# Attention scores: queries and keys as two fp32r parts in the lower and upper half of the array's rows, issued in pairs of heads

## The chip, the cores and the metric

One core of a Trainium2 chip runs the whole program. The metric is the device time of one execution in microseconds (us). A matmul here is an instruction of TensorE (PE): it multiplies a stationary operand, loaded first by a weight load (PEld), with a moving operand that streams through, and writes into one of eight PSUM banks. VectorE (DVE), ScalarE (ACT) and GpSimd (POOL) do the rest, SyncE (SP) issues most DMAs.

## The reference

Two independent results are put side by side: an attention with a memory over four segments, and a filter in the frequency domain (a real 2-D FFT of 2048 x 576, a product with a complex weight, and the inverse).

```python
q,k,v = x@wq, x@wk, x@wv            # 2048 x 576, 32 heads of 18, segments of 512
for s in range(4):
    qs, ks, vs = q[:, :, s], k[:, :, s], v[:, :, s]
    logits = einsum("bhqd,bhkd->bhqk", qs, ks) * scale + mask    # causal within the segment
    p = softmax(logits); a_dot = einsum("bhqk,bhkd->bhqd", p, vs)
    pq = phi(qs); num = pq @ M; den = (pq . z) + 1e-6
    outs.append(g * num / den + (1 - g) * a_dot)
    pk = phi(ks); M += pk^T vs; z += sum(pk)
a = concat(outs) @ wo
b = irfft2(rfft2(x2) * (w_r + 1j*w_i))
```

Everything is asked for in fp32. The kernel gets there by splitting operands into parts that TensorE takes in one pass and summing the products of the parts.

## The kernel before, in words

The program is written out in one order for all engines; each engine runs its own instructions in that order. It has these stages: the forward transform; the projections (`projections`, with the middle of the transform on DVE between its steps); the inverse transform, with a `prologue` of the attention beside it; the attention loop (`attention`, line 928 on); the last projection.

**Projections.** For each of 4 segments nine units `qk_unit` (line 467) make 128 rows of q and k each: 14 matmuls of width 512 (line 464) into a PSUM bank `pj`, then the result is split into three bf16 parts in `sp3` (three buffers): a copy on ACT (477), a subtraction on DVE in PSUM (484), a second copy on ACT (488), and the rest either by a subtraction on DVE (490, 18 units) or by a matmul with a negative identity `nid` and a third copy on ACT (492, 493, 18 units). A DMA on SP's queue writes the three parts to DRAM (`qkD`, line 494). Four `v_unit` per segment follow.

**Stacks.** For eight heads (a group n of 16) `stack_dmas` loads six pieces of 18 rows each for q and for k: q as parts 0,0,0,1,1,2 and k as 0,1,2,0,1,0, so that one matmul over 108 rows sums the six products of parts that matter. Rows 108 and 109 hold the row maxima (for q) and -1 (for k). There are three q and four k buffers.

**Scores.** A step t of the attention loop is one head: quad k = t//4, head hh = t%4 in it. Scores are made twice. `s1` (line 636) makes them with queries on the partitions for the head t+10: four matmuls (widths 384, 128, 512, 256) and one bf16 matmul that adds the causal mask to two diagonal blocks; DVE takes row maxima from them (648, 654). `mpath` turns the maxima of four heads by a transpose on PE (674) and a small DMA into rows 108 and 109 of q. `s2` (line 680) makes the scores again with keys on the partitions for the head t, maxima already subtracted, and ACT takes the exponential (689, 694, 698); POOL masks the diagonal blocks after every fourth head (701). `s1` and `s2` are generators of three steps each, which the loop calls in turn, with other work between them: `pv` (line 718, P times V, in 32-column strips), and in some stages of the loop the memory products (`mem1`, `combine`) and the output projection (`oproj`, line 861) from a queue `bg`. PSUM banks: three for `s1`, three for `s2`, one `pv`, one `post`. The prologue makes `s1` of the first ten heads.

What sets the order around the change: the order in which the loop calls these generators, the rings of three PSUM banks, and SP's queue for the stack loads, of which the loop takes two per step.

## Time and profile before

| | |
|---|---|
| timed runs | 707.5, 711.49, 711.28 us (median 711.28) |
| profiled execution | span 709.2 us from its first to its last instruction; the page gives no other time of it |
| granted TensorE clock | 0.997 |
| HBM | 81.78 MB read, 38.24 MB written |
| DMA share of the span | hardware queue 51.8%, software queue 8.2% |

Busy times are sums of durations, and matmuls overlap, so the distance between the starts of neighbouring instructions tells the cost of one better than its duration. Rows of a timeline give the start in us, the duration, the engine, the line, what is written and read and the shape; a bracket says how long the engine was idle before and what ended it. Rows of windows give the stretch, its length, and then for each engine the busy time with the number of instructions, the granted clock, the DMA share and GB/s.

### The profile page before, as it was taken

The page shows a single profiled execution, that of the slowest core. Times are in us where ns is not written, and L with a number is a line of the kernel's source. Part 1 is how long each engine was busy: PE and PEld are TensorE (multiplying, and loading weights), DVE is VectorE, ACT ScalarE, POOL GpSimd, SP SyncE. Part 2 cuts the span into 40 slices and gives each one's busy share as a digit, 9 for nine tenths or more (in the row PEclk, how much of TensorE's full clock was granted, in tenths as well). Part 3 has the DMA queues.
Part 4 walks back from the last instruction along what each step waited for, and adds up shares of the span by engine and source line. Part 5 has one row for each costly group of instructions (what it writes and reads, how often), then busy time and mean ns, then how long its engine had stood idle before and what let it go on. Part 6 is the DMA issues. An engine that isn't in the chain of part 4 may idle for free.

```text
span 709.2 us, 14168 instructions
## 1 busy us (share of the span) xinstructions
PE 676.4 (95%) x4861; PEld 498.7 (70%) x4861; DVE 556.2 (78%) x1233; ACT 441.0 (62%) x994; POOL 208.8 (29%) x409
## 2 busy tenths in 40 slices
PE   4999999999999999999999899999999999998997
PEld 4999779889879888999844444444566445764677
DVE  6999999899989889887588688877666876568153
ACT  3657695574574563444388677777666676567741
POOL 2110000100100111565165334555233753246210
PEclk9999999999999999999999999999999999999999
DMA  9876546555563568899647666676556765441331
GB/s 343 272 233 205 150 141 194 175 178 167 165 211 133 165 215 279 201 239 211 180 109 176 172 161 154 173 181 169 128 129 185 171 164 128 122 129 52 99 100 69
DMA packets 83388, 121.04 MB, mean 171 GB/s; under 512 B 11368, under 2 KB 50902, under 8 KB 83180
## 3 DMA queue, kind: packets, MB, share of 16 engines
q1 hardware_dynamic: 76724, 104.11, 51.8%
q0 software_dynamic: 6592, 16.03, 8.2%
q8 instruction: 38, 0.62, 0.4%
q14 instruction: 34, 0.28, 0.1%
HBM read 81.78 MB, written 38.24 MB: 169 GB/s over the span
## 4 chain that ended last, share of the span: by engine, by line
PE 61%; DVE 9%; DMA 6%; ACT 5%; issue 3%; POOL 3%; DVEq 0%; SPq 0%; ACTq 0%; POOLq 0%
PE pv L718 9%; PE po L861 7%; PE pj L464 6%; PE pjv L464 6%; PE s L644 5%; PE i L300 4%; PE i L311 4%; PE s L652 3%; PE s L688 3%; PE po L892 2%; DVE junk L648 2%; PE s L692 2%; PE pn L791 2%; PE pm L524 2%; PE s L653 2%
## 5 line engine op out<-in xcount | busy, mean ns | idle before, releaser
L648 DVE CUSTOM_DVE_ANT_0 junk<-s,mask 128x512 bf16<-128x512 f32 (+1 forms) x256 | 141.8, 554 | 55.1 <-PE s L644 44.3
L654 DVE TENSOR_REDUCE mx<-s 128x4 f32<-128x512 f32 x128 | 87.9, 687 | 20.0 <-PE s L653 18.2
L689 ACT ACTIVATE P<-s 128x512 f32<-128x512 f32 x128 | 77.2, 603 | 24.1 <-PE s L688 20.9
L718 PE MATMUL pv<-P,vs 128*32 128x512 f32 (+3 forms) x1024 | 82.3, 440 | 0.0
L694 ACT ACTIVATE P<-s 128x512 f32<-128x512 f32 x128 | 77.1, 602 | 6.9 <-PE s L693 3.8
L698 ACT ACTIVATE P<-s 128x256 f32<-128x256 f32 x128 | 49.6, 387 | 49.7 <-PE s L697 49.6
L701 POOL TENSOR_SCALAR_AFFINE_SELECT P<-P 128x512 f32<-128x512 f32 x116 | 69.4, 635 | 5.6 <-ACT P L689 4.7
L718 PEld LDWEIGHTS pv<-P,vs 128*32 128x32 f32 x1024 | 26.9, 109 | 45.0 <-issue 42.9
L464 PE MATMUL pj<-x,wqkh 128*128 128x512 f32 x162 | 56.1, 407 | 0.0
L210 DVE TENSOR_TENSOR t<-Z 128x580 f32<-128x580 f32 x64 | 46.7, 757 | 0.2
L514 POOL MEMSET vt<- 128x32 f32 x16 | 2.4, 159 | 148.8 <-PE pm L524 121.5
L210 DVE TENSOR_TENSOR Z<-t 128x580 f32<-128x580 f32 x64 | 45.9, 756 | 0.0
L644 PE MATMUL s<-Ks,Qs 108*128 108x512 bf16 (+1 forms) x128 | 42.2, 330 | 0.0
L488 ACT CAST sp<-pj 128x512 bf16<-128x512 f32 x36 | 21.1, 585 | 30.7 <-DVE pj L484 30.7
L142 PE MATMUL f<-ftab,eh 128*128 128x290 f32 (+1 forms) x160 | 31.6, 317 | 9.0 <-DMA ftab<-ftab 9.0
L300 PE MATMUL i<-civ,Y 128*128 128x256 f32 (+1 forms) x288 | 37.9, 284 | 1.6 <-DVE T L332 1.6
L300 PEld LDWEIGHTS i<-civ,Y 128*128 128x128 f32 (+1 forms) x288 | 35.8, 181 | 1.8 <-DVE T L332 1.8
L311 PE MATMUL i<-itab,T 128*128 128x290 f32 (+1 forms) x224 | 36.4, 312 | 0.0
L464 PEld LDWEIGHTS pj<-x,wqkh 128*128 128x128 f32 x162 | 30.4, 188 | 8.4 <-issue 1.7
L669 POOL CAST mh<-mg 128x16 bf16<-128x16 f32 x32 | 6.8, 214 | 99.1 <-ACT mg L667 67.9
L464 PE MATMUL pj<-xh,wqkh 128*128 128x512 f32 x90 | 35.6, 395 | 0.0
L464 PE MATMUL pj<-xh,wqkl 128*128 128x512 f32 x90 | 35.6, 395 | 0.0
(214 smaller groups left out, 1859.6 us busy)
## 6 DMA issues: line engine op xcount, KB each, us to landing
qkD<-sp SPq DMA_DIRECT2D x36, 384.0 KB
Ks<-qkD SPq DMA_DIRECT2D x72, 144.0 KB
x<-qkD SPq DMA_DIRECT2D x60, 144.0 KB
Qs<-qkD SPq DMA_DIRECT2D x60, 144.0 KB
xin<-xb SPq DMA_DIRECT2D x16, 384.0 KB
cfw<-cfw POOLq DMA_DIRECT2D x16, 384.0 KB, 4.5
civ<-civ POOLq DMA_DIRECT2D x16, 384.0 KB, 7.5
vs<-vD SPq DMA_DIRECT2D x16, 330.0 KB
```

The lines of the kernel that those rows point to most:

```text
L210: v.tensor_tensor(o,a,b,op=op)
L300: nc.tensor.matmul(p[:m,k],Y[i][:,q,c*128:c*128+m],cc[:,hl,o:o+256],start=n==0,stop=n==5)
L311: nc.tensor.matmul(p,x,t,start=n==0,stop=n==6)
L464: s.nc.tensor.matmul(out,a,b,start=i==0,stop=i==len(L)-1)
L644: nc.tensor.matmul(out,Q[:108,h,128*i:128*i+128],K[:108,h,:128*(i+1)],start=True,stop=True)
L648: nc.vector.tensor_tensor_reduce(out=junk[:,:w],in0=src,in1=s.mask[:,512-w:],scale=1.0,scalar=-3.0e38, op0=OP.add,op1=OP.max,accum_out=s.m ...
L654: nc.vector.tensor_reduce(out=s.mx[k][:,hh],in_=pa.rearrange("p (b c) -> p b c",c=128),axis=mybir.AxisListType.X,op=OP.max)
L689: nc.scalar.activation(P[0][:,hh],p0,AF.Exp,scale=SC)
L694: nc.scalar.activation(P[1][:,hh],p1,AF.Exp,scale=SC)
L701: if k<29: nc.gpsimd.affine_select(out=x,in_=x,pattern=pat+[[1,128]],compare_op=OP.is_ge,fill=0.0,base=0,channel_multiplier=-1)
L718: nc.tensor.matmul(s.pvt[32*hh:32*hh+32,128*j:],vt[:,j,19*h:19*h+32],mv[0][:,hh,mv[1]],start=j==0,stop=j==2,skip_group_check=True)
L861: nc.tensor.matmul(ps,a[t][:r,c],b[:r,t,w],start=i==0,stop=i==14)
```

## The change

q and k are split into two fp32r parts instead of three bf16 parts, with one copy on ACT and one subtraction on DVE; the `nid` matmuls, the second and third copies are gone. `sp` has two buffers of 4 KB per partition instead of three of 3 KB. A stack now has three pieces of 18 rows (q parts 0,0,1; k parts 0,1,0), 54 rows, plus two for maxima and -1. The first quad of a group lies in rows 0 to 55, the second in rows 64 to 119, and pieces of four heads are loaded instead of eight (as many DMAs of as many bytes). The scores of head t (`s2` before, B) and of head t+12 (`s1` before, A; t+10 before) always lie in different halves of the rows; `pair` issues their four products in turn, B and A of equal width, 512, 384, 128 and 256, then the mask product, then ACT's and DVE's work on them. `pv` and the background steps come after a whole pair. `mpath` starts after the quad's fourth head and its transpose follows the next pair; its PSUM bank is now that of `pv`. The prologue makes A alone for twelve heads.

```diff
-        s.qkD=[d(f"qkD{i}",[1152,3,512],BF) for i in range(4)]
+        s.qkD=[d(f"qkD{i}",[1152,2,512],F32) for i in range(4)]
...
-    def third(s,g,mt): return g>0 and mt%3
     def qk_unit(s,g,mt,tp,pp):
...
         ps=pp.tile([128,512],F32,name="pj",tag="pj")
         yield from s.passes(ps,g,"wqk",slice(128*mt,128*mt+128),slice(0,512),False)
         yield
-        sp3=tp.tile([128,3,512],BF,name="sp3",bufs=3)
+        sp=tp.tile([128,2,512],F32R,name="sp",bufs=2)
...
-        nc.scalar.copy(sp3[:,0],ps)
...
+        nc.vector.tensor_tensor(sp[:,1],ps,sp[:,0].bitcast(F32),op=OP.subtract)
         if r1>r0: nc.vector.scalar_tensor_tensor(e[r0:r1],ps[r0:r1],0.0,e[r0:r1],op0=OP.max,op1=OP.add)
-        nc.vector.tensor_tensor(ps,ps,sp3[:,0],op=OP.subtract)
         qr=min(r1,128 if mt<4 else (64 if mt==4 else 0))
         if qr>r0: nc.sync.dma_start(s.pqD[g][128*mt:128*mt+qr],e[:qr])
         yield
-        nc.scalar.copy(sp3[:,1],ps)
-        yield
-        if s.third(g,mt): nc.vector.tensor_tensor(sp3[:,2],ps,sp3[:,1],op=OP.subtract)
-        else:
-            nc.tensor.matmul(ps,s.nid,sp3[:,1],start=False,stop=True,skip_group_check=True)
-            nc.scalar.copy(sp3[:,2],ps)
-        nc.sync.dma_start(s.qkD[g][128*mt:128*mt+128],sp3)
+        nc.sync.dma_start(s.qkD[g][128*mt:128*mt+128],sp.bitcast(F32))
...
-        s.nid=wv.tile([128,128],BF,name="nid"); s.nc.scalar.activation(s.nid,s.ident,AF.Copy,scale=-1.0)
...
-                w=tot/(36-18*.3+12*2.7+4*2.0)*((2.7 if g<3 else 2.0) if i>8 else .7 if s.third(g,i) else 1.0)
+                w=tot/(36+12*2.7+4*2.0)*((2.7 if g<3 else 2.0) if i>8 else 1.0)
...
-        s.Qs+=[cp.tile([128,8,512],BF,name=f"Qs{i}") for i in range(1,3)]
-        s.Ks+=[cp.tile([128,8,512],BF,name=f"Ks{i}") for i in range(1,4)]
+        s.Qs+=[cp.tile([128,4,512],F32R,name=f"Qs{i}") for i in range(1,3)]
+        s.Ks+=[cp.tile([128,4,512],F32R,name=f"Ks{i}") for i in range(1,4)]
...
-        t=pool.tile([128,18,512],BF,name="x0",tag="x0",bufs=1)
-        s.Qs,s.Ks=[t[:,:8]],[t[:,8:16]]; s.loaded=set()
+        t=pool.tile([128,9,512],F32R,name="x0",tag="x0",bufs=1)
+        s.Qs,s.Ks=[t[:,:4]],[t[:,4:8]]; s.loaded=set()
...
+    def stack_dmas(s,n,qk,halves=(0,1)):
 
...
-        T,base,order=((s.Qs[n%3],0,(0,0,0,1,1,2)),(s.Ks[n%4],576,(0,1,2,0,1,0)))[qk]
-        for pc,o in enumerate(order):
-            a=s.qkD[g][base+8*G*18:base+8*G*18+18,o]
-            ap=bass.AP(tensor=a.tensor,offset=a.offset,ap=[[1536,18],[1536*18,8],[1,512]])
-            def go(T=T,pc=pc,ap=ap):
-                nc.sync.dma_start(T[18*pc:18*pc+18],ap)
-                if pc==5: s.loaded.add((n,qk))
-            L.append(go)
+        T,base,order=((s.Qs[n%3],0,(0,0,1)),(s.Ks[n%4],576,(0,1,0)))[qk]
+        for qd in halves:
+            for pc,o in enumerate(order):
+                a=s.qkD[g][base+(8*G+4*qd)*18:base+(8*G+4*qd)*18+18,o]
+                ap=bass.AP(tensor=a.tensor,offset=a.offset,ap=[[1024,18],[1024*18,4],[1,512]])
+                def go(T=T,r=64*qd+18*pc,ap=ap,pc=pc,qd=qd):
+                    nc.sync.dma_start(T[r:r+18].bitcast(F32),ap)
+                    if pc==2: s.loaded.add((2*n+qd,qk))
+                L.append(go)
         return L
...
-    def s1(s,t):
...
+    def pair(s,a,b):
+
+        nc=s.nc; A=[];B=[]
...
+            k,hh=divmod(a,4); n,qd=divmod(k,2); r=64*qd
+            assert (k,0) in s.loaded and (k,1) in s.loaded,a
+            Q,K=s.Qs[n%3][r:r+54,hh],s.Ks[n%4][r:r+54,hh]
...
+            pc,pa=[s.ps1.tile([128,512],F32,name="s1",tag="s1") for _ in range(2)]; pb=s.ps1.tile([128,256],F32,name="s1",tag="s1")
+            A=[(pc,3,512,True),(pa[:,:384],2,384,True),(pa[:,384:],0,128,False),(pb,1,256,True)]
+            A=[(o,Q[:,128*i:128*i+128],K[:,:w],f) for o,i,w,f in A]
...
+            u,hb=divmod(b,4); n,qe=divmod(u,2); r=64*qe
+            q,kk=s.Qs[n%3][r:r+56,hb],s.Ks[n%4][r:r+56,hb]
...
+            p0,p1=[s.ps.tile([128,512],F32,name="s2",tag="s2") for _ in range(2)]; p2=s.ps.tile([128,256],F32,name="s2",tag="s2")
+            B=[(p0,0,128*0),(p1[:,:384],1,128),(p1[:,384:],3,384),(p2,2,256)]
+            B=[(o,kk[:,128*j:128*j+128],q[:,c:],True) for o,j,c in B]
+        for i in range(4):
+            for L in (B,A):
+                if not L: continue
+                o,x,y,f=L[i]
+                nc.tensor.matmul(o,x,y,start=f,stop=L is B or i in (0,3),skip_group_check=True)
+        if A:
+            nc.tensor.matmul(pa[:,256:].rearrange("p (a c) -> p a c",a=2),s.idb,s.tri[:,None,:].to_broadcast([128,2,128]),start=False,stop=True,skip_group_check=True)
+        if B:
+            nc.scalar.activation(P[0][:,hb],p0,AF.Exp,scale=SC)
+            nc.scalar.activation(P[1][:,hb],p1,AF.Exp,scale=SC)
+            nc.scalar.activation(P[2][:,hb],p2,AF.Exp,scale=SC)
+        if A:
+            def red(src,i):
+                w=128*(i+1)
+                junk=s.sm.tile([128,512],BF,name="junk",bufs=1)
+                nc.vector.tensor_tensor_reduce(out=junk[:,:w],in0=src,in1=s.mask[:,512-w:],scale=1.0,scalar=-3.0e38,
+                    op0=OP.add,op1=OP.max,accum_out=s.mg[k][:,hh,i:i+1])
+            red(pc,3); red(pb,1)
+            nc.vector.tensor_reduce(out=s.mx[k][:,hh],in_=pa.rearrange("p (b c) -> p b c",c=128),axis=mybir.AxisListType.X,op=OP.max)
+        if B and hb==3:
+            def sel(x,pat):
...
-        p,a=(s.ps,"post") if 1<k<10 else (s.psm,s.mtag)
-        pt=p.tile([128,1024],BF,name="mt",tag=a)[:,:128]
+        pt=s.psm.tile([128,1024],BF,name="mt",tag=s.mtag)[:,:128]
         nc.tensor.transpose(pt,mh.rearrange("p a m -> p (a m)"),s.idb)
         yield
         mt=s.sm.tile([32,128],BF,name="mts",bufs=1)
         nc.scalar.copy(mt,pt[:32])
-        nc.gpsimd.dma_start(Q[108:110,4*qd:4*qd+4].rearrange("p h (i c) -> p (h i) c",c=128),mt)
...
+        a="post" if s.now<117 else "s1" if s.now<131 or name=="po" else "s2"
...
-        i=0
-        for t in range(10):
-            for _ in s.s1(t):
-                for _ in range(1+(i%24==0)):
-                    if q: q.pop(0)()
-                i+=1
+        m=None
+        for t in range(12):
+            s.pair(t,None)
+            if 2<=t<6:
+                for r in (54,118): nc.gpsimd.dma_start(s.Ks[t-2][r:r+2].rearrange("p h c -> p (h c)"),io["neg1"][:,:2048])
+            for i in range(3):
+                if q: q.pop(0)()
+                if m is not None and i<2: next(m,None)
                 yield
-            if 2<=t<6: nc.gpsimd.dma_start(s.Ks[t-2][108:110].rearrange("p h c -> p (h c)"),io["neg1"])
-            if t in (3,7): m=s.mpath(t//4); next(m)
-            if t in (4,8): next(m); next(m,None)
-        assert not q
+            m=None
+            if t%4==3: m=s.mpath(t//4); next(m)
+        while q: q.pop(0)()
+        if m is not None:
+            for _ in m: pass
...
-        nc=s.nc; s.tp,s.ps,s.psm,s.mtag=tp,ps,s.ps1,"s1"
+        nc=s.nc; s.tp,s.ps,s.psm,s.mtag=tp,ps,ps,"pv"
...
-            if hh==0 and qd==0:
-                if 0<n<14: q+=s.stack_dmas(n+2,0)
-                if 0<n<13: q+=s.stack_dmas(n+3,1)
-                if n+2<16: q.append(lambda n=n: s.load_v(n+2))
+            if hh==0 and k>0:
+                if k+5<32: q+=s.stack_dmas((k+5)//2,0,((k+5)%2,))
+                if k+7<32: q+=s.stack_dmas((k+7)//2,1,((k+7)%2,))
+            if hh==0 and qd==1 and n+2<16: q.append(lambda n=n: s.load_v(n+2))
...
-            a=s.s1(t+10) if t+10<128 else iter(())
-            b=s.s2(t) if t<128 else iter(())
             if q: q.pop(0)()
             if qu: qu.pop(0)()
-            if hh==3 and m is not None: steps(m,1)
-            steps(a,1)
-            steps(b,1)
+            if t<128: s.pair(t+12 if t+12<128 else None,t)
+            if hh==0 and m is not None: steps(m,1)
             r=(t-5)%4
+            if 5<=t<129: s.pv((t-5)//4,(t-5)%4)
+            if hh==3 and k+3<32: m=s.mpath(k+3); next(m)
             if r%2: run_bg(1)
-            steps(a,1)
-            steps(b,1)
-            if 5<=t<129: s.pv((t-5)//4,(t-5)%4)
+            if hh==0 and m is not None: steps(m,1)
...
-            steps(a,1)
-            steps(b,1)
-            if hh==2 and m is not None: steps(m,1)
-            if hh==1 and k+2<32: m=s.mpath(k+2); next(m)
```

PE in the quiet part of the attention loop (`idb` and `tri` make the mask product, `s` are score banks, `x` is the first q or k stack). Before, from the mask product of one head to the P·V of a quad:

```order
L653 LDWEIGHTS idb
L653 MATMUL s_5022<-tri,idb 128x256
L688 LDWEIGHTS Ks_3179
L688 MATMUL s_5027<-Qs_3177,Ks_3179 128x512 [waits Activation_49]
L644 LDWEIGHTS x_2655
L644 MATMUL s_5030<-Ks_3180,x_2655 128x512 [waits DVE_49]
L692 LDWEIGHTS Ks_3179
L692 MATMUL s_5034<-Qs_3177,Ks_3179 128x384 [waits Activation_49]
L693 LDWEIGHTS Ks_3179
L693 MATMUL s_5034<-Qs_3177,Ks_3179 128x128
L718 MATMUL pv<-P_4852,vs 32x512 [waits Pool_49]
L718 MATMUL pv<-P_4852,vs 32x512 x3
```

Each product has a weight load of its own, and first scores (644, 652) and second scores (688 to 697) take turns; P·V stands before the last two products of the head. Now, one head and the P·V after it:

```order
L653 MATMUL s_4897<-Qs_3081,Ks_3083 128x512 [waits Activation_49]
L653 MATMUL s_4894<-Ks_3084,x_2583 128x512 [waits DVE_49]
L653 MATMUL s_4898<-Qs_3081,Ks_3083 128x384 [waits Activation_49]
L653 MATMUL s_4895<-Ks_3084,x_2583 128x384 [waits DVE_49]
L653 MATMUL s_4898<-Qs_3081,Ks_3083 128x128
L653 MATMUL s_4895<-Ks_3084,x_2583 128x128
L653 MATMUL s_4899<-Qs_3081,Ks_3083 128x256 [waits Activation_49]
L653 MATMUL s_4896<-Ks_3084,x_2583 128x256 [waits DVE_49]
L655 LDWEIGHTS idb
L655 MATMUL s_4895<-tri,idb 128x256
L702 MATMUL pv<-P_4652,vs 32x384 x4
L702 MATMUL pv<-P_4653,vs 32x256 x4
```

The weight loads of fp32r products aren't listed by the program, but they are part of the products. Eight products of two heads stand together, B's products of widths 512, 384 and 256 wait for ACT and A's for DVE, and P·V has moved behind them.

ACT in the projections, in the first segment (lines with - before, with + now):

```order
-L488 CAST sp_1055<-pj 128x512
-L477 CAST sp_1092<-pj 128x512
-L493 CAST sp_1055<-pj 128x512
+L476 CAST sp<-pj 128x512
 L408 CAST wvh<-raw 128x288 x2
 L435 CAST xh<-xst 128x512
-L488 CAST sp_1092<-pj 128x512
-L477 CAST sp_1130<-pj 128x512
-L493 CAST sp_1092<-pj 128x512
+L476 CAST sp<-pj 128x512
```

Per unit there were three copies and now there is one.

The transpose of the maxima on PE. Before:

```order
L697 LDWEIGHTS Ks_3179
L697 MATMUL s_4939<-Qs_3177,Ks_3179 128x256 [waits Activation_49]
L674 LDWEIGHTS mh [waits Pool_49]
L674 MATMUL mt<-idb,mh 128x128
L652 LDWEIGHTS x_2655
L652 MATMUL s_4951<-Ks_3180,x_2655 128x384 [waits DVE_49]
```

Now:

```order
L655 LDWEIGHTS idb
L655 MATMUL s_4941<-tri,idb 128x256
L687 LDWEIGHTS mh [waits Pool_49]
L687 MATMUL mt<-idb,mh 128x128 [waits Activation_49]
L653 MATMUL s_4978<-Qs_3081,Ks_3083 128x512 [waits Activation_49]
L653 MATMUL s_4975<-x_2583,Qs_3080 128x512 [waits DVE_49]
```

Both times it stands one head after the fourth head of its quad. Before, POOL's part (`mh`) was written two heads after the masking of the second scores' quad (line 701); now it is written right behind that masking, in the step before this transpose.

67 lines of the change are left out of this document (13 added, 54 removed).

## The prediction

> **What bounds the kernel now.** I read the page first (shares by engine), then the windows by stage, then the timeline of PE and DVE in one stretch, because the shares average over stages.
>
> ```profile
> span 709.2 us, 14168 instructions
> PE 676.4 (95%) x4861; PEld 498.7 (70%) x4861; DVE 556.2 (78%) x1233; ACT 441.0 (62%) x994; POOL 208.8 (29%) x409
> ```
>
> PE is nearly always busy. The attention (351 to 674 us) falls into three kinds of stages. The first fence has the busy time by engine (PE, PEld, DVE, ACT, POOL); the second has line 689 alone, the first exponential of a head, so its count is the number of heads in the stage.
>
> ```profile
> 351.10:458.20 107.10, 100.70 (x842) 49.23 (x840) 88.07 (x272) 81.29 (x198) 50.71 (x97) 0.98 0.65 159
> 458.20:501.00 42.80, 40.27 (x305) 18.55 (x303) 33.64 (x95) 30.70 (x72) 20.31 (x35) 1.00 0.68 166
> 501.00:545.90 44.90, 44.77 (x369) 30.30 (x369) 27.21 (x77) 28.00 (x67) 15.53 (x32) 1.00 0.59 144
> ```
>
> ```profile
> 351.10:458.20 107.10, 30.42 (x50) 0.98 0.65 159
> 458.20:501.00 42.80, 9.58 (x16) 1.00 0.68 166
> 501.00:545.90 44.90, 8.39 (x14) 1.00 0.59 144
> ...
> 559.00:591.30 32.30, 7.17 (x12) 1.00 0.67 169
> 591.30:635.70 44.40, 8.36 (x14) 1.00 0.48 128
> ```
>
> Two heads take 4.28 us in the quiet stage (107.1/25), 5.35 and 5.38 where the memory products are mixed in, 6.41 and 6.34 where the output projection is. In the quiet stage PE (94%) and DVE (82%) are both close to their limit; in the last kind PE is full and DVE 61% busy. So time taken from PE pays fully in the projection stages, partly in the mixed ones, and in the quiet ones only down to what DVE allows. One quiet head on PE:
>
> ```profile
> 408.57 1.28 PE L718 MATMUL pv<-P,vs 128*32 128x384 f32 x16
> 409.79 0.28 PE L644 MATMUL s<-x,Qs 108*128 108x256 bf16 x1
> 409.91 0.28 PE L697 MATMUL s<-x,Ks 110*128 110x256 bf16 x1
> 410.02 0.38 PE L652 MATMUL s<-x,Qs 108*128 108x384 bf16 x2
> 410.25 0.27 PE L653 MATMUL s<-tri,idb 128*128 128x256 bf16 x1
> 410.36 0.38 PE L688 MATMUL s<-x,Ks 110*128 110x512 bf16 x1
> 410.57 0.38 PE L644 MATMUL s<-x,Qs 108*128 108x512 bf16 x1
> 410.79 0.33 PE L692 MATMUL s<-x,Ks 110*128 110x384 bf16 x1
> 410.96 0.22 PE L693 MATMUL s<-x,Ks 110*128 110x128 bf16 x1
> 411.01 0.27 PE L644 MATMUL s<-x,Qs 108*128 108x256 bf16 x1
> 411.12 0.27 PE L697 MATMUL s<-x,Ks 110*128 110x256 bf16 x1
> 411.30 0.38 PE L652 MATMUL s<-x,Qs 108*128 108x384 bf16 x2
> ```
>
> The second column overlaps from row to row, so the cost is the distance between starts. From 410.02 to 411.30 is a head: 0.23 + 0.11 + 0.21 + 0.22 + 0.17 + 0.05 + 0.11 + 0.11 = 1.21 of products, and some 0.07 of waiting before 411.30. The P·V group takes 1.22 (408.57 to 409.79). DVE's part of a head:
>
> ```profile
> 410.56 0.69 DVE L654 TENSOR_REDUCE mx<-s 128x4 f32<-128x512 f32 x1
> 411.16 0.68 DVE L648 CUSTOM_DVE_ANT_0 junk<-s,mask 128x512 bf16<-128x512 f32 x1
> 411.77 0.08 DVE L648 DVE_READ_ACCUMULATOR2_ANT mg<- 128x1 f32 x1
> 412.00 0.42 DVE L648 CUSTOM_DVE_ANT_0 junk<-s,mask 128x256 bf16<-128x256 f32 x1
> 412.35 0.08 DVE L648 DVE_READ_ACCUMULATOR2_ANT mg<- 128x1 f32 x1
> ```
>
> 0.60 + 0.69 + 0.43 = 1.72 us, and the change leaves all of it.
>
> **The price of a pair.** The trace has no fp32r product in half the rows, so I build it from three kinds of rows: fp32r streams, two weight loads that follow each other, and the only 64-row products.
>
> ```profile
> 130.84 3.31 PE pj L464 x14
> ...
> 291.07 1.41 PE i L300 x12
> ```
>
> ```profile
> 199.66 0.40 PE L464 MATMUL pj<-x,wqkh 128*128 128x512 f32 x1
> 199.99 0.46 PE L501 MATMUL ptr<-ident,ex 64*128 64x64 f32 x4
> 200.38 0.49 PE L464 MATMUL pj<-x,wqkh 128*128 128x512 f32 x1
> 200.71 0.40 PE L464 MATMUL pj<-x,wqkl 128*128 128x512 f32 x1
> ```
>
> ```profile
> 204.09 0.19 PEld L464 LDWEIGHTS pj<-x,wqkh 128*128 128x128 f32 x1
> ...
> 204.19 0.19 PEld L464 LDWEIGHTS pj<-x,wqkl 128*128 128x128 f32 x1
> ```
>
> An fp32r product takes 0.236 at width 512 (3.31/14) and 0.118 at 256 (1.41/12); at 384 and 128 I take the same rate, 0.177 and 0.059. Weight loads follow at 0.10. Into the 64-row products and out again PE loses 0.33 - 0.236, about 0.09, each time. The Trainium skill, TensorEngine Tiling (Array Packing), Key Properties, says that changing the tiling mode drains TensorE, which speaks against a change that switches twice per head; the rows agree with about 0.09 each, and without the rule the pair below would be 0.19 cheaper and the sum, over the 56 heads of the busy stages, 10.6 lower.
>
> Lower bound, the two halves at once: a stage lasts as long as one product, or as one load at width 128: 0.236 + 0.177 + 0.10 + 0.118 = 0.63; with the mask product 0.11 and two changes of mode 0.19 it is 0.93. Middle, with loads one behind the other: eight at 0.10 or a little more, 0.84, + 0.30 = 1.14. Upper bound, nothing overlaps: 2 x 0.63 + 0.30 = 1.56. The nearest row is the P·V group, four column strips of the array:
>
> ```profile
> 547.39 0.16 PEld L718 LDWEIGHTS pv<-P,vs 128*32 128x32 f32 x8 [0.21 <-issue]
> ```
>
> Eight loads of 32 columns lie inside 0.16; one behind the other, at 0.10 for 128 columns, they would need 0.20. So loads to different strips overlap, and the sixteen fp32 instructions of the group fit into 1.22. I take 0.93: 0.28 less than 1.21. The Trainium skill, TensorE: Matmul & The Clock Gate, Part 3 (row/col tiling), says that products in different row groups run concurrently and gives 3.07 for four of them; no row here shows it for row groups. By it the sum is the one below, without it the first rival's.
>
> **The sum, part by part.**
>
> Projections. Gone are 18 `nid` products, a copy on ACT per unit, 18 third copies on ACT and 18 subtractions on DVE.
>
> ```profile
> 195.41 0.40 PE L464 MATMUL pj<-x,wqkh 128*128 128x512 f32 x1
> 196.40 0.38 PE L492 MATMUL pj<-sp,nid 128*128 128x512 bf16 x1 [0.59 <-ACT sp L488]
> ```
>
> 18 x 0.22 is 4.0, and this one wait 0.6. The freed DVE and ACT time lies beside PE; I give it 1 more. Together -5.5. What could eat it: `sp` has two buffers instead of three and its write grows from 384 to 512 KB. A unit is about 3.6 us, so a buffer must be copied, split and written within 7.2; since two links of the old chain are gone I count nothing, up to +8 if ACT then waits for the write.
>
> Before the attention. Twelve heads of the first scores alone instead of ten, beside the full inverse transform: 12 x 0.93 (no partner shortens them) against 10 x 0.66 (0.23 + 0.11 + 0.22 + 0.11 less rounding) is +4.6; the two heads leave the attention, -1.3. +3.3.
>
> Quiet stage. Here PE's order counts more than its sum. A head's four products are now issued in one go, and all three banks of the first scores are taken again by the next head. Where P·V stands between pair t and pair t+1 the chain is: the last reduction of the head before ends and frees the bank of the second stage; PE's stages two to four, the change of mode and the mask product, 0.18 + 0.10 + 0.12 + 0.09 + 0.11 = 0.60; P·V with its entry 1.22 + 0.09; the first product of the next head, 0.38 until DVE may read it (the row at 410.57); DVE 1.72. That is 4.01 for two heads, about 4.15 with some four hand-overs by semaphore (an estimate). Before it was 4.28, but PE is idle for 6.4 us of the stage (107.1 less 100.7); without these 4.03. I leave the idle time in and count 0.12 x 25 = +3; bounds -3 (the idle time goes too) and +10. Also the transpose of the maxima now follows the pair right after the masking of the same quad's end on POOL:
>
> ```profile
> 357.35 2.39 POOL L701 TENSOR_SCALAR_AFFINE_SELECT P<-P 128x512 f32<-128x512 f32 x4
> ```
>
> The queued `mh` work behind these 2.39 us makes PE wait, and the next pair behind it: mostly hidden by DVE's 1.72; I take 0.1 per four heads, +1. The quiet stage is +4.
>
> Mixed and projection stages. There PE has other work after each pair, so banks are free in time. 28 heads of the one (16 + 12) and 28 of the other (14 + 14) at 0.28 less: -7.8 each. Bounds: nothing, and -10 each if the waits inside them shrink too.
>
> Tail. The last twelve heads have second scores alone: 0.63 + 0.19 against 0.55 (0.21 + 0.17 + 0.05 + 0.11), +3.2, and the four paired heads before them -1.1. +2.
>
> The stack loads keep their number and bytes (three of four heads for six of eight) and are asked for earlier; nothing. Sum: -5.5 + 3.3 + 4 - 7.8 - 7.8 + 2 = -11.8. The profiled execution spans 709.2; the page gives no time around it, and the median of the runs is 711.28, 2.1 more. So 711.28 - 11.8 = 699.5, say 699.
>
> **The rivals.** First, the two halves don't overlap for fp32r (a pair of 1.56, 0.35 more than before). For it: no row shows row groups at once. Against it: the column strips do. Price: mixed and projection +9.8 each, quiet chain +0.46 per two heads (0.22 in stages two to four, 0.24 in the first), +11.5 + 4; with the rest (-5.5 + 3.3 + 2) it is +35: 746. Second, products overlap and loads don't (1.14): the big stages give -2 each, the quiet chain gets 0.24 longer, +6 + 4; sum about +6: 717, within 1%. For it: fp32r loads at 0.10 apart on PEld; against it: the eight loads in 0.16. Third, on the slower side too, the burst itself: with one set of three banks for each kind of score, PE stands in front of a held bank also in the mixed stages, so that each pair of heads costs 0.5 more than I have, in 39 pairs of heads +20, sum +8: 719. It decides as soon as other work on PE after a pair is shorter than about 1.1 us (1.72 + 0.38 on DVE less 0.93), which the quiet heads without P·V are; for it speaks DVE's 82% there, against it that P·V and projections fill most others.
>
> **How the numbers follow.** Forecast 0.48, its own range 686 to 710 (projections -4 to -10, quiet -4 to +10, big stages -8 to -20). No overlap 0.20 (735 to 755), loads apart 0.18 (708 to 722), burst 0.14 (710 to 725). A measurement of this kernel tells about 1% from no change, so faster is below 704: nearly all of the forecast and a little of the second, 0.48; within 1%: the second, part of the third and the end of the first, 0.22; slower 0.30. The range 684 to 742 leaves out about half of the no-overlap case and a tenth of the forecast.
>
> **What would show it.** Right: in the timeline the lower and upper product of one stage start at nearly the same time; a pair, first start to mask product, about 0.8; two heads of the projection stages at 5.8; about 4.2 in the quiet ones, with DVE idle after P·V. Wrong: starts 0.2 apart at width 512 (no overlap) or PEld rows 0.10 apart with PE waiting (loads); ACT waiting for the `qkD` write; PE waiting for `mh` for more than 0.5 us each time.

## The result, and the profile after

The changed kernel takes 766.70 us (median of 4 runs, 765.74 to 768.81) against 710.38 us (707.5 to 711.49): 1.0787 times as long, with a 95% interval of 1.0744 to 1.0829. I had forecast 699 with a range of 684 to 742. The time lies above the range and on the other side. Where executions of one kernel lie more than 1.5% apart, the time and the ratio given below are those of the faster ones, and the others are named beside them.

The head of the page of the changed kernel, the line on PE's granted clock with it:

```profile
span 767.1 us, 14190 instructions
PE 702.8 (92%) x4843; PEld 528.2 (69%) x4843; DVE 549.9 (72%) x1215; ACT 413.6 (54%) x939; POOL 209.8 (27%) x413
PEclk9999999999999999989899999988999998996899
```

The kernel before has a 9 in all forty slices. Its mean granted clock is 0.997, that of the changed kernel 0.949. Since the clock has only the values 1.00 and 0.50 in these traces, 0.949 means that 78 us of the 767.1 (twice 0.051) ran at half speed, against some 4 us before.

The windows by stage show where the time went. The columns are busy time of PE, PEld, DVE, ACT and POOL, then granted clock, DMA share and GB/s. The stages are: projections; inverse transform with the first heads' scores; heads 0 to 47; then 16, 16, 16, 16 and 12 heads, the stages with memory products and those with the output projection taking turns. First the kernel before:

```profile
0.00:276.20 276.20, 262.85 (x1567) 232.97 (x1568) 251.66 (x413) 167.89 (x345) 26.11 (x92) 1.00 0.63 203
276.20:351.20 75.00, 73.35 (x571) 69.35 (x571) 56.11 (x130) 33.23 (x83) 34.77 (x52) 1.00 0.81 205
351.20:454.60 103.40, 97.00 (x808) 47.36 (x807) 84.84 (x260) 78.40 (x191) 50.32 (x97) 0.98 0.64 158
454.60:495.10 40.50, 38.04 (x294) 18.24 (x292) 32.87 (x94) 29.54 (x70) 19.47 (x33) 1.00 0.70 171
495.10:545.90 50.80, 50.61 (x413) 32.46 (x412) 31.11 (x89) 32.01 (x76) 16.76 (x36) 1.00 0.60 145
545.90:585.80 39.90, 37.43 (x292) 18.05 (x289) 32.24 (x93) 29.29 (x69) 24.27 (x36) 1.00 0.69 168
585.80:635.80 50.00, 49.64 (x404) 31.81 (x405) 31.26 (x90) 31.49 (x75) 17.71 (x38) 1.00 0.49 130
635.80:663.30 27.50, 25.36 (x214) 14.06 (x213) 18.68 (x45) 21.51 (x51) 14.29 (x20) 1.00 0.13 39
```

The same stages, head for head, in the changed kernel:

```profile
0.00:270.60 270.60, 258.71 (x1548) 231.06 (x1548) 241.68 (x394) 140.38 (x288) 26.39 (x90) 1.00 0.67 224
270.60:366.50 95.90, 85.03 (x581) 79.46 (x581) 59.94 (x140) 34.72 (x86) 37.77 (x62) 0.93 0.66 164
366.50:478.10 111.60, 101.87 (x811) 54.90 (x808) 86.00 (x261) 78.28 (x190) 49.14 (x94) 0.94 0.62 156
478.10:528.50 50.40, 42.43 (x298) 21.16 (x294) 33.98 (x94) 29.64 (x70) 19.32 (x34) 0.86 0.55 139
528.50:582.80 54.30, 49.21 (x406) 32.52 (x408) 30.20 (x88) 31.20 (x76) 16.64 (x37) 0.97 0.52 134
582.80:628.20 45.40, 37.56 (x297) 19.10 (x295) 33.53 (x93) 29.47 (x70) 23.87 (x35) 0.96 0.55 141
628.20:684.10 55.90, 49.79 (x408) 32.46 (x404) 31.14 (x89) 30.59 (x75) 17.93 (x40) 0.94 0.41 107
684.10:719.30 35.20, 34.26 (x203) 21.20 (x199) 15.97 (x34) 21.57 (x49) 13.35 (x17) 0.71 0.11 31
```

Read them row against row: -5.6 in the projections, +20.9 before the attention, +8.2 in the quiet heads, +9.9, +3.5, +5.5 and +5.9 in the four stages with other work, +7.7 in the last heads; what follows takes 1.9 more. Together +57.9, the difference of the spans. Two columns moved: PE is idle in stages where it was full (8.0 of 50.4 us in the first mixed stage, 2.5 of 40.5 before), and the clock fell, most of all in the last stage, where PE is busy to 97% and yet 7.7 us slower. Over the whole execution PE is idle 31.5 us more than before (64.3 against 32.8) and busy 26.4 us more (702.8 against 676.4).

The pair itself does what I had priced. One of them in PE's timeline (start, duration, engine, line, operation; then active rows by columns of the array):

```profile
419.65 0.50 PE L653 MATMUL s<-x,Ks 56*128 56x512 f32 x1
419.65 0.50 PE L653 MATMUL s<-x,Qs 54*128 54x512 f32 x1
419.99 0.34 PE L653 MATMUL s<-x,Ks 56*128 56x384 f32 x1
419.99 0.34 PE L653 MATMUL s<-x,Qs 54*128 54x384 f32 x1
...
420.49 0.28 PE L655 MATMUL s<-tri,idb 128*128 128x256 bf16 x1
```

Both products of a stage start in the same hundredth of a microsecond, and the four stages with the change of mode behind them take 0.84 us. With 0.11 for the mask product that is 0.95, against my 0.93. The loss is not in the pair but around it. Who PE waited for, from the list of waits (total, times, longest):

```profile
PE mt L687 <- POOL mh L684: 19.6, 15, 2.8
...
PE pn L775 <- DVE am L782: 4.4, 3, 1.8
PE po L845 <- ACT ob L847: 3.4, 7, 0.5
PE i L300 <- ACT vt L510: 2.6, 1, 2.6
```

The first row is the transpose of the maxima (1.0 us in all in the kernel before). The rows of `pn`, `pb`, `pd` and `po`, nine in the list, come to 19.4 us; before they were six rows and 3.7. With the 2.6 us at the start of the inverse transform PE stood some 37 us longer in these rows. The first transpose in PE's timeline, and POOL's work ahead of it:

```profile
306.58 0.90 PE L653 MATMUL s<-x 54*128 54x512 f32 x4
307.42 0.28 PE L655 MATMUL s<-tri,idb 128*128 128x256 bf16 x1
310.49 0.29 PE L687 MATMUL mt<-idb,mh 128*128 128x128 bf16 x1 [2.79 <-POOL mh L684]
310.54 3.63 PE L311 MATMUL i<-itab,T 128*128 128x290 f32 x14
```

```profile
307.55 1.82 POOL L285 TENSOR_TENSOR Y<-Z,Y 128x512 fp32r<-128x512 f32 x2 [1.71 <-ACT Y L284]
309.31 0.61 POOL L270 DMA_DIRECT2D civ<-civ  x1
309.92 0.21 POOL L683 CAST mh<-mg 128x16 bf16<-128x16 f32 x1
310.22 0.21 POOL L684 TENSOR_TENSOR mh<-mg,mh 128x16 bf16<-128x16 f32 x1
```

PE came to the transpose one pair after the maxima were asked for, and POOL first had 1.82 us of the inverse transform and a DMA to issue. What follows the stand costs more: fourteen products of width 290 take 3.63 us instead of 2.15 (the same products in prologue_filler below). The windows around this place, and around the last heads, in the changed kernel:

```profile
307.09:310.50 3.41, 0.62 (x5) 0.30 (x5) 2.52 (x8) 0.73 (x3) 2.72 (x5) 1.00 0.97 186
310.50:313.91 3.41, 3.41 (x15) 3.41 (x16) 0.00 (x0) 0.66 (x2) 1.67 (x3) 0.50 1.05 183
692.79:696.20 3.41, 2.63 (x19) 1.43 (x22) 1.89 (x3) 3.01 (x8) 3.15 (x5) 1.00 0.14 24
696.20:716.68 20.48, 20.48 (x94) 13.09 (x86) 6.21 (x9) 10.30 (x23) 6.20 (x6) 0.50 0.11 33
```

A stretch of 3.41 us with PE mostly idle is followed by one at half clock. In the last heads the stretch ahead has PE busy for 2.63 of 3.41 us, and the half clock then stays for 20.48 us although PE is busy in all of them. The kernel before had shown a half clock once in the attention, and windows of 10 us that I had in hand, with clocks of 0.89 and 0.94, pointed at it:

```profile
394.29:397.70 3.41, 1.35 (x16) 0.69 (x9) 0.86 (x6) 0.60 (x3) 0.41 (x2) 1.00 0.62 164
397.70:401.12 3.42, 3.42 (x17) 1.59 (x18) 2.84 (x8) 2.56 (x6) 1.24 (x2) 0.50 0.63 178
```

There PE stood once for a DMA, 2.1 us, and the next 3.42 us ran at 0.50, and then the clock was back.

### The profile page after: what moved, and what is told of

Its sections match the earlier page's. It is cut to its first block, busy times and chain, and to the rows that moved or that the text cites. A ratio compares the mean times of both kernels' runs of the same rounds, so it can differ in the third digit from the quotient of the medians.

```text
span 767.1 us, 14190 instructions
## 1 busy us (share of the span) xinstructions
PE 702.8 (92%) x4843; PEld 528.2 (69%) x4843; DVE 549.9 (72%) x1215; ACT 413.6 (54%) x939; POOL 209.8 (27%) x413
## 4 chain that ended last, share of the span: by engine, by line
PE 35%; POOL 6%; DVE 5%; ACT 4%; issue 2%; DMA 1%; DVEq 0%; POOLq 0%; ACTq 0%
PE s L653 10%; PE pv L702 9%; PE po L845 7%; POOL P L670 4%; DVE junk L664 2%; PE po L876 2%; PE pn L775 2%; PE s L655 2%; DVE mx L667 1%; DMA x<-mts 1%; ACT P L657 1%; PE pd L756 1%; POOL ol L798 1%; PE i L311 1%; PE mt L687 1%
## 5 line engine op out<-in xcount | busy, mean ns | idle before, releaser
L670 POOL TENSOR_SCALAR_AFFINE_SELECT P<-P 128x512 f32<-128x512 f32 x125 | 76.5, 643 | 140.8 <-ACT P L657 115.3
L702 PE MATMUL pv<-P,vs 128*32 128x512 f32 (+3 forms) x1024 | 91.8, 481 | 0.4 <-ACT mts L690 0.4
L653 PE MATMUL s<-Ks,Qs 54*128 54x512 f32 (+3 forms) x256 | 69.4, 373 | 1.6 <-DVE mx L667 0.4
L653 PEld LDWEIGHTS s<-Qs,Ks 56*128 56x128 f32 x256 | 45.1, 198 | 35.2 <-issue 16.4
L653 PE MATMUL s<-Qs,Ks 56*128 56x512 f32 (+3 forms) x256 | 66.0, 372 | 2.1 <-ACT P L657 1.6
L476 ACT CAST sp<-pj 128x512 fp32r<-128x512 f32 x36 | 21.1, 585 | 62.9 <-DMA qkD<-sp 28.6
L464 PE MATMUL pj<-x,wqkh 128*128 128x512 f32 x162 | 54.3, 399 | 0.0
L653 PEld LDWEIGHTS s<-Ks,Qs 54*128 54x128 f32 x256 | 45.1, 197 | 7.4 <-DVE mx L667 4.6
L300 PEld LDWEIGHTS i<-civ,Y 128*128 128x128 f32 (+1 forms) x288 | 37.6, 193 | 3.8 <-ACT vt L510 2.8
L311 PE MATMUL i<-itab,T 128*128 128x290 f32 (+1 forms) x224 | 37.4, 323 | 0.0
L655 PE MATMUL s<-tri,idb 128*128 128x256 bf16 x128 | 37.2, 291 | 0.0
```

Source lines behind the costliest of these rows:

```text
L300: nc.tensor.matmul(p[:m,k],Y[i][:,q,c*128:c*128+m],cc[:,hl,o:o+256],start=n==0,stop=n==5)
L464: s.nc.tensor.matmul(out,a,b,start=i==0,stop=i==len(L)-1)
L653: nc.tensor.matmul(o,x,y,start=f,stop=L is B or i in (0,3),skip_group_check=True)
L655: nc.tensor.matmul(pa[:,256:].rearrange("p (a c) -> p a c",a=2),s.idb,s.tri[:,None,:].to_broadcast([128,2,128]),start=False,stop=True,skip ...
L670: if u<29 or x.tensor is not P[0].tensor: nc.gpsimd.affine_select(out=x,in_=x,pattern=pat+[[1,128]],compare_op=OP.is_ge,fill=0.0,base=0,ch ...
L702: nc.tensor.matmul(s.pvt[32*hh:32*hh+32,128*j:],vt[:,j,19*h:19*h+32],mv[0][:,hh,mv[1]],start=j==0,stop=j==2,skip_group_check=True)
```

## The experiments

Theory: the pair is as fast as priced, and the time went into three things around it: the stand before the transpose, stands between slots of other work that now follow each other, and the half clock that comes after. Rivals to it: the three banks of each kind of score couple PE and DVE (my third rival), or DVE takes the gain. In all kernels of the pair below the projections take 270 to 272 us as in the changed kernel; where stages are named, sixteen quiet heads are heads 16 to 31 of the attention, from exponential to exponential.

### The transpose one head later (late_transpose, late_transpose_b)

```diff
-            if t<128: s.pair(...)
-            if hh==0 and m is not None: steps(m,1)
+            if hh==1 and m is not None: steps(m,2)
+            if t<128: s.pair(...)
```

(In the prologue the transpose moves two slots back as well, and the third one into the loop.) In the loop this puts the transpose behind the other work that follows the same pair. In the quiet heads no product stands there, so that the order on PE, pair, transpose, pair, is the same as in the changed kernel.

> The transpose of the maxima stands one head later (one slot group later before the attention), so that the masks and the casts on POOL are done when PE comes to it; products, pairs and reductions are unchanged. Theory (PE stands before the transpose, 19.6 us in all, and each stand of 2 to 3 us is followed by 3.4 us or more at half clock): the waits for mh fall below 3 us, the stretches at half clock from 75 us to about 45, and the time from 766.7 to 730-742. Rival (the pairs' banks set the pace, the wait only moves into the next pair): 757-767, with the time that leaves the transpose standing before the score products.

> The kernel of late_transpose once more, for its rows: if the stand before the transpose was what left, the waits for mh are below 10 us in all (19.6 in the changed kernel), the longest below 1.5 us, and the stretches at half clock come to 40-55 us; if it only moved, PE's waits for DVE's reductions have grown by about as much.

Measured: 739.01 us (median of three), 1.0372 (1.0310 to 1.0434) times the kernel before; late_transpose_b, the same kernel, 742.31 in its one execution. (A fourth execution of late_transpose took 3152 us with PE's products more than four times as long; it is left out, and the rows are those of late_transpose_b.) The row of the waits:

```profile
PE mt L687 <- POOL mh L684: 2.7, 4, 1.5
```

The mean clock is 0.968, so 47 us at half speed instead of 78. The gain of 24 to 28 us is more than the 17 us of stands that went: the 31 us less at half speed, worth up to 15, are in it. The stage before the attention went from 95.9 to 81.6 us. The 2.7 us that are left lie in heads 0 to 47, where PE's order did not change: 4.2 us there in the changed kernel, and the stage took 113.2 us instead of 111.6. The theory holds for the other stages, at the slow end of what I gave; for the quiet heads this kernel doesn't test it.

### Dummy products in the stand (prologue_filler)

```diff
+        if k<3:
+            fl=s.psm.tile([128,512],F32,name="fl",tag=s.mtag)
+            for i in range(8): nc.tensor.matmul(fl...,s.idb,s.tri...,start=True,stop=True,...)
         pt=s.psm.tile([128,1024],BF,name="mt",tag=s.mtag)[:,:128]
```

> As the changed kernel, with eight dummy products of full size (128 rows and columns, width 512, bf16, 1.76 us together, written over by the transpose that follows) ahead of the first three transposes, where PE stands for 2.8, 2.8 and 2.0 us. The stand itself keeps its length, only now PE is busy in it. Theory (the half clock behind a stand is a cost of its own): the stretches at half clock at 310.5 (3.4 us) and 334.4 (6.8 us) go, and the time falls by 4 to 6 us to 761-763. Rival (behind the stand PE waits for DVE and ACT anyway, so that the clock costs nothing): 766-769.

Measured: 750.09 and 759.60 us (1.0595; 1.0483 to 1.0708), the other two 761.96 and 765.53. These lie further apart than the gain that I looked for, so the rows decide; they are those of the execution of 761.96 us. The same place in PE's timeline:

```profile
307.43 1.89 PE L688 MATMUL fl<-tri,idb 128*128 128x512 bf16 x8
310.39 0.23 PE L690 MATMUL mt<-idb,mh 128*128 128x128 bf16 x1 [1.07 <-POOL mh L684]
310.43 2.15 PE L311 MATMUL i<-itab,T 128*128 128x290 f32 x14
```

The transpose starts where it did (310.39, before 310.49), only PE worked 1.89 of the 2.8 us. The fourteen products behind it take 2.15 us instead of 3.63. Over the stretch from 300 to 360 us, first the changed kernel, then this one:

```profile
300.00:360.00 60.00, 52.47 (x353) 48.84 (x352) 38.75 (x94) 20.48 (x51) 23.66 (x38) 0.91 0.67 161
```

```profile
300.00:360.00 60.00, 57.63 (x405) 50.68 (x404) 39.65 (x97) 21.31 (x53) 25.00 (x41) 1.00 0.68 168
```

The stage before the attention takes 91.6 us instead of 95.9. So products of no use in the stand saved 4.3 us there, at the low end of my 4 to 6: the half clock is a cost of its own, beside the stand. (The profiled executions differ by 6.9 us; the rest lies in heads behind, where the two kernels are alike.)

### The last heads over 120 rows (tail_full_rows)

```diff
-            q,kk=s.Qs[n%3][r:r+56,hb],s.Ks[n%4][r:r+56,hb]
+            if a is None: r=0
+            h_=r+56 if a is not None else 120
+            q,kk=s.Qs[n%3][r:h_,hb],s.Ks[n%4][r:h_,hb]
```

(Four fills with zeros on POOL, ahead of the inverse transform's products, clear the rows between the two halves.)

> As the changed kernel, but the last twelve heads' second scores, which have no partner, run over 120 rows of the array instead of 56: they then add two heads' products, so their values are not the reference's (and four memsets stand on POOL before the inverse transform's products). Number, widths and order of the products stay. Theory (the clock gate counts the cells of the array that work, not time: with 56 rows alone the last stage stays below the limit): the 20.5 us at half clock from 696 to 717 go and the stage from there to the end is 8 to 10 us shorter, 757-760 in all. Rival (the gate goes by the waits of PE alone): the stretch at half clock stays and the time is 765-769.

Measured: 756.17 us (1.0624; 1.0550 to 1.0698). The stage of the last twelve heads:

```profile
679.70:705.70 26.00, 24.80 (x203) 15.74 (x200) 16.56 (x34) 21.24 (x50) 14.55 (x17) 1.00 0.15 42
```

26.0 us instead of 35.2, with the clock at 1.00 instead of 0.71, with the same number of products of the same widths. That is what the theory gave, with one reserve: late_order and late_slots below came through the same heads with 56 rows at full clock (26.8 and 28.8 us), late_transpose_b, spread_pv and late_order_masks did not (35.3, 35.4, 37.4). So half rows don't close the gate by themselves; they keep it from opening once it is closed. It also means that 7 to 10 us between two kernels below can come from the last heads alone. What decides is told at the end, worked out over sixteen traces.

### The slots of other work apart (late_slots)

On late_transpose:

```diff
+            r=(t-5)%4
+            if r%2: run_bg(1)
             if t<128: s.pair(...)
-            r=(t-5)%4
             if 5<=t<129: s.pv((t-5)//4,(t-5)%4)
             if hh==3 and k+3<32: m=s.mpath(k+3); next(m)
-            if r%2: run_bg(1)
```

> As late_transpose, and in the heads that have two slots of other work the first slot stands ahead of the pair instead of behind it. Theory (in the changed order both slots of a head follow each other at once, so that the chain from a memory product over DVE or ACT to the next product in the same bank is uncovered; in late_transpose PE stands 16 us before such products): these waits fall below 8 us, sixteen heads of the mixed stages from 45 to 41-43 us, and the time from 739-742 to 727-734. Rival (the other work is held elsewhere, or the clock gate gives the time back): the mixed stages stay at 44-46 and the time at 737-745.

Measured: 721.89 us (median of three; the fourth execution took 740.28; 1.0153; 1.0098 to 1.0208), the best so far. The stages of the first mixed heads and of the output projection beside them:

```profile
461.60:503.40 41.80, 39.14 (x299) 19.90 (x297) 33.37 (x94) 29.55 (x72) 20.07 (x35) 1.00 0.70 173
503.40:551.60 48.20, 46.89 (x407) 32.19 (x407) 30.71 (x88) 30.35 (x75) 15.71 (x34) 1.00 0.56 151
```

The waits of `pn`, `pb`, `pd` and `po` are down to 6.1 us; the mixed stages take 41.8 and 43.9, the projection stages 48.2 and 49.0, below the 50.8 and 50.0 of the kernel before. The mean clock is 0.987. It came out below what I expected, because the last heads kept the full clock (28.8 against 35.3 us in late_transpose_b). That is 6.5 of the 20.4 us between the two profiled executions, in a stage for which I had named no gain.

### The banks' order, the masks, P·V inside the pair (late_order, late_order_masks, split_pair)

```diff
-            A=[(pc,3,512,True),(pa[:,:384],2,384,True),(pa[:,384:],0,128,False),(pb,1,256,True)]
+            A=[(pc,3,512,True),(pb,1,256,True),(pa[:,:384],2,384,True),(pa[:,384:],0,128,False)]
...
-            B=[(p0,0,128*0),(p1[:,:384],1,128),(p1[:,384:],3,384),(p2,2,256)]
+            B=[(p0,0,128*0),(p2,2,256),(p1[:,:384],1,128),(p1[:,384:],3,384)]
```

(The exponentials follow the order of the banks.)

> As late_transpose, and in a pair the widths go 512, 256, 384, 128 and the reductions in the order in which the banks are filled (c, b, a), so that the bank that DVE frees first is the one PE needs next. Theory (PE and DVE hold each other up over the three banks, some 0.3 to 0.5 us per head beside DVE's 1.72): 10 to 25 us below late_transpose, 710-728, and DVE's waits for the score products fall from 65 us to below 45. Rival (the three banks of the second scores and the exponentials hold the pair, or the quiet heads are at DVE's limit anyway): within 5 us of late_transpose.

Measured: 741.84 us (1.0415; 1.0350 to 1.0481). No gain: the rival. The order of the banks was not a loss.

> As late_order, with the four masks of a finished quad behind the two casts of mh on POOL instead of ahead of them (2.4 us). Theory (the transpose still stands for POOL, 8.4 us in late_order, and some stretches at half clock follow from it): the waits for mh fall below 2 us and the time by 6 to 12 us, to 730-736. Rival (the masks are then late for P.V, which waits instead): no gain or a loss, 740-746, with waits of P.V for POOL.

Measured: 751.51 us (1.0570; 1.0504 to 1.0636). The waits for `mh` are down to 0.2 us, but P·V now stands 3.5 us for the copy of the transposed maxima, and the time is worse. The two profiled executions differ by 10.1 us, and the last heads alone took 37.4 us against 26.8, so what the masks' new place is worth is not shown.

> As late_order_masks, and P.V and one of the two slots of other work stand inside the pair, between its products of widths 512, 256 and those of 384, 128, instead of behind it. Theory (behind P.V DVE has nothing to reduce for about 0.7 us in each two heads, because the whole pair must be issued in one go and P.V behind it; PE in turn stands before the last bank): sixteen quiet heads take 30-33 us instead of 36-39, DVE's waits for score products fall from 72 to below 50 us, and the time is 700-718. Rival (the exponentials and the three banks of the second scores hold the pair, or the clock gate takes the gain): 728-742, sixteen quiet heads still 35 or more.

```diff
+            next(pr,None)
             r=(t-5)%4
             if 5<=t<129: s.pv((t-5)//4,(t-5)%4)
+            if r%2: run_bg(1)
+            for _ in pr: pass
```

Measured: 759.06 us, the other three 774.85 to 779.03; sixteen quiet heads took 40.8 us in the execution of 759.06. My theory of the burst behind the pair gives the wrong sign here. With P·V in its middle, the pair's last bank comes 1.2 us late, and DVE waits 69 us for that bank (and 20 for the others), against 73 for all in late_order_masks.

### P·V spread over three heads (spread_pv, spread_slots, spread_slots_mt)

```diff
-        for j in ((0,3),(),(1,2),())[jj]:
+        for j in ((0,),(1,),(3,2),())[jj]:
```

> As late_order, with the P.V products of a quad spread over three heads (widths 512; 384; 128 and 256) instead of two bursts of 1.22 us behind every second pair. Theory (behind the burst DVE runs dry for 0.7 us because the next pair comes 1.22 us late, and the banks let nothing be issued ahead): with at most 0.5 us behind a pair the 1.72 us of DVE cover it; sixteen quiet heads take 29-33 us instead of 36-40, and the time is 715-729 against 739-742. Rival (the second scores' banks and the exponentials, or the clock gate, hold the pair): 35 us or more for sixteen quiet heads, 735-745.

> Both edits, the slot ahead of the pair and P.V over three heads, on late_order. Theory (two separate losses): the gains add, 703-718. Rival (one of the two was no loss): as the better of the two alone, or 735 and more if neither was.

> As spread_slots, with the transpose one head later again and in a bank of the first scores. Theory (with P.V spread only the stand before the transpose and what the gate adds keep the quiet heads from DVE's pace): the waits for mh fall from 13.6 to below 3 us, sixteen quiet heads take 30-34 us, 705-718 in all. Rival (pairs at DVE's pace leave the array too few cells at work, and the gate takes the gain; or the transpose in a score bank holds the next pair): 722-740, with 25 us or more at half clock.

Measured: 745.67 (1.0496), 726.94 (1.0255; 1.0175 to 1.0336) and 734.76 us (1.0332). The slots are worth 19 us once more (745.67 to 726.94), of which 7.1 lie again in the last heads (35.4 against 28.3). P·V's spread brings nothing that shows in the time, so all three theories miss and their rivals come out: in spread_pv heads 0 to 47 take 112.1 us against 115.1 in late_order, but the last heads 35.4 against 26.8; in spread_slots heads 0 to 47 take 113.9 against 108.9 in late_slots. Sixteen quiet heads took 33.8, 34.9 and 35.6 us, near the 34.4 of late_slots and the 35.2 of the kernel before. Where P·V is spread, the stand before the transpose is 11.2 and 13.6 us (8.4 in late_order, on which these kernels build); that POOL has less time for the masks there is my reading. Where the transpose is moved once more (spread_slots_mt) it is gone, and PE instead stands 8.9 us for the exponentials, which hold the second scores' banks behind ACT's copies of the maxima and of P·V.

### The casts on DVE (spread_slots_dve, late_slots_dve)

```diff
-        nc.gpsimd.tensor_copy(mh[:,0],mg)
-        nc.gpsimd.tensor_tensor(mh[:,1],mg,mh[:,0],op=OP.subtract)
+        nc.vector.tensor_copy(mh[:,0],mg)
+        nc.vector.tensor_tensor(mh[:,1],mg,mh[:,0],op=OP.subtract)
```

(The copy ahead of them moves from ACT to DVE too.)

> As spread_slots, with the two casts of mh (and the copy ahead of them) on DVE right behind its reduction of the maxima, instead of on POOL behind the masks. Theory (with P.V spread, the quiet heads run at DVE's pace and only the stand before the transpose, 11.7 us in the quiet stage of spread_slots, and the half clock behind such stands keep them from it): the waits for the transpose's input fall below 2 us, sixteen quiet heads take 30-33 us instead of 35-40, the stretches at half clock fall from 34 us to below 20, and the time is 704-715, level with the kernel before. Rival (DVE is the bound and pays for the casts, 0.3 us in each quad, or the gate closes all the same because pairs at DVE's pace keep too few cells at work): 720-730.

> As late_slots, with the same casts on DVE. The waits for mh are only 2.9 us there, because P.V in bursts gives POOL the time. Theory (the stand is what the casts on POOL cost): little to gain, 717-723, sixteen quiet heads 34-38 us as in late_slots (P.V's burst holds them). Rival (POOL's masks and casts also delay P.V and the exponentials): 705-715.

Measured: 775.46 (1.0923; 1.0886 to 1.0960) and 746.92 us (1.0544; 1.0492 to 1.0597), the largest misses. The casts don't cost the 0.3 us per quad that I had counted. DVE's rows and POOL's at one quad of spread_slots_dve:

```profile
450.30 0.54 DVE L683 CAST mh<-mg 128x16 bf16<-128x16 f32 x1
450.87 0.55 DVE L684 TENSOR_TENSOR mh<-mg,mh 128x16 bf16<-128x16 f32 x1
```

```profile
448.85 2.55 POOL L670 TENSOR_SCALAR_AFFINE_SELECT P<-P 128x512 f32<-128x512 f32 x4 [6.80 <-ACT P L657]
```

Sixteen columns take 0.54 and 0.55 us while POOL is at its masks; over the 32 casts and the 32 subtractions the medians are 0.52 and 0.55 us, the shortest 0.17 each. DVE is held for about a microsecond in most quads, the pairs wait for it, and the clock does the rest: its mean is 0.918, and heads 0 to 47 run at 0.80 and take 130.7 us (113.9 in spread_slots). The Trainium skill, SBUF — State Buffer, section "SBUF: two separate sides", says that VectorE and GpSimd share one pair of ports, which is an exclusive lock for a whole instruction, for VectorE in some modes or with two inputs from SBUF; these rows agree.

### Reductions cut short, in both kernels (late_slots_short, before_short)

```diff
-                w=128*(i+1)
+                w=128; src=src[:,:128]
...
-            nc.vector.tensor_reduce(out=s.mx[k][:,hh],in_=pa.rearrange("p (b c) -> p b c",c=128),...)
+            nc.vector.tensor_reduce(out=s.mx[k][:,hh],in_=pa.rearrange("p (b c) -> p b c",c=128)[:,:,:32],...)
```

> As late_slots, with the three reductions of a head cut to a quarter or half of their columns (128 of 512, 128 of 256, 32 of each 128), so that the maxima are not the reference's and DVE's part of a head falls from 1.72 us to about 0.8. Theory (behind the shorter pair DVE is the bound: late_slots has DVE at 80% in its quiet and mixed stages, which is where the 0.28 us per head saved on PE went): sixteen quiet heads fall from 34-39 us to 26-30, the mixed ones from 42-44 to 35-39, the time from 723 to 675-700. Rival (the banks, the exponentials or the clock gate hold the pair): 712-725, and the stages within 2 us of late_slots.

> The kernel before with the same shorter reductions (the maxima are not the reference's). Theory (PE bounds it: 1.21 + 0.61 us per head against DVE's 1.72): sixteen quiet heads fall from 34.5 us by at most 5, to 29.5-32.5, the time from 711 to 685-700, and late_slots_short is the faster of the two by 5 to 20 us, as my sum had it for pairs that nothing else holds. Rival (the pairs themselves are no faster): late_slots_short and before_short differ as late_slots and the kernel before do, +10 to +14 us.

Measured: 713.78 us (1.0053; 1.0000 to 1.0106) and 708.08 us (0.9972; 0.9935 to 1.0010). My theory that DVE had become the bound falls: without more than half of its reductions late_slots gains some 8 us, not 23 or more, and is still not faster than the kernel before cut in the same way. Of the 11 us between late_slots and the kernel before, some 5 go, 6 stay, which neither my theory nor its rival had. In before_short sixteen quiet heads fell from 35.2 to 31.7 us, as I had expected where PE is the bound, but heads 64 to 79 took 5.8 us longer (a wait of 2.7 us for a DMA, a clock of 0.94); in late_slots_short the quiet ones fell only from 34.4 to 33.7. From 352 to 460 us, the quiet heads of late_slots_short:

```profile
352.00:460.00 108.00, 94.76 (x831) 51.91 (x830) 44.54 (x263) 78.49 (x193) 50.14 (x97) 0.94 0.69 172
```

PE 88%, ACT 73%, DVE 41%: no engine is full. Here PE stands 6.6 us before the transpose, in ten of these heads' quads, and 5.1 us before P·V for ACT's copy of the transposed maxima, in four, and the clock is at 0.94. What remains is the chain of one quad (masks, casts, transpose, copy, P·V) and the gate behind it. I made no kernel that took the whole chain apart, so how the loss divides between the two stays open. By stages the 11 us between the profiled executions of late_slots and the kernel before are -5.8 in the projections, +7.3 before the attention (+3.3 was forecast, and 2.6 is the stand at the start of the inverse transform), +5.5 in the quiet heads, +1.7 in the four stages with other work, +1.3 in the last heads and +1.0 behind them.

## Why the prediction was wrong

The step that failed is the price of what stands around the pair. The sum took PE's waits there as hidden or filled (+1 us for the transpose, nothing in the mixed and projection stages) and had no term for the clock. The runs show some 37 us of new stands and some 37 us of clock lost.

**The projections** were right: -5.5 forecast, -5.6 measured. ACT did wait for the write of 512 KB from two buffers, which I had named as a sign of being wrong: 28.6 us in 13 waits, 0.6 before. But PE has no row of waits for ACT's copies in `pj`, so it cost nothing that shows.

**The price of the pair** was right: the halves overlap, products and weight loads alike, and the two rivals on that point (746 and 717) did not happen. That 746 lies nearer to the result is no merit of its mechanism.

**"The transpose follows the pair right after the masking", +1 us**: the mechanism was the right one and the size was off by nearly twenty. I took 0.1 us per four heads as mostly hidden by DVE. It was 19.6 us, up to 2.8 at a time and 1.3 on average (more than 0.5 each time was my sign of being wrong). In the quiet heads, which alone the +1 was for, it was 4.2 us; 7.8 us fell into the four stages with other work, and 7.5 before the attention, where I had not looked and where the inverse transform's subtractions stand ahead on POOL. "Before the attention" became +20.9 instead of +3.3: the forecast 3.3, the 7.5, the 2.6 at the start of the inverse transform and a lost clock of 0.07 x 95.9 = 6.7 us come to 20.1.

**The mixed and projection stages**, -7.8 each, were +15.4 and +9.4. The step that failed is "there PE has other work after each pair, so banks are free in time". The banks were; the other work was not ready. In the kernel before, products of the scores stand between the two slots of a head; with the pair issued in one go the slots touch, and a memory product's result must pass ACT or DVE before the next one may use the bank. late_slots shows it: moving one slot ahead of the pair took these waits from 21.5 us (late_transpose_b) to 6.1.

**What the sum lacked altogether is the clock.** I priced every stand at its own length. Of the three stands at the transposes ahead of the attention, those of 2.79 and 2.77 us were followed by 3.4 and 6.8 us at half clock; the third, 1.97 us up to 359.48, was not: it lies across the edge of two stretches of 3.41 us (358.3), so that PE was busy for 77% and 65% of them. Worked out from the clock column, the six stages of the attention and the one before lost 0.07 x 95.9 + 0.06 x 111.6 + 0.14 x 50.4 + 0.03 x 54.3 + 0.04 x 45.4 + 0.06 x 55.9 + 0.29 x 35.2 = 37 us of full clock, against 2 before. That is an upper bound of its cost, because PE was not the bound everywhere. With some 37 us of new stands it gives 74 above my forecast of -12, where +57.9 was measured, 70 above. Both figures are upper bounds, so this is agreement in size: the two together are enough for the miss. That the half clock costs time beside the stands, prologue_filler (4.3 us) and tail_full_rows (9.2 us in the last heads) show.

**The third rival** (the burst, 719) had the sign, but no run bears out its mechanism: neither another order of the banks (late_order) nor another place or length of P·V (split_pair, spread_pv) brought the time back. That the last heads alone can move a time by 7 to 10 us limits what these three tell.

**The quiet heads** (+4 forecast, +8.2 measured) are +5.5 in late_slots (108.9 against 103.4), once transposes and slots are mended. That this is near the forecast is partly luck, for the clock there is 0.94 (0.98 before), which the forecast didn't have. The best version that computes the same, 721.89 us, stays 1.5% slower than the kernel before; no version of the pair beat it.

## What to carry to other kernels

A step that makes TensorE's work shorter can be worth nothing until the work that waits for its results has been moved along: list for each product that leaves its old place which two dependent steps now touch, and which engine's queue stands between them. Price a stand of TensorE at its length and, if the traces show it, at the slow clock behind it; here the single stall in the profile of before (2.1 us, then 3.42 us at 0.50) would have told it. And when TensorE's share falls, look at the granted clock first: fewer cells at work can make every product that is left slower.
